# A view of its own for each indirect store of result rows, in an attention, expert and feed-forward kernel on one core

## The chip, the core and the metric

The kernel runs on one core of a Trainium2 chip. The metric is the device time of one execution in microseconds (us), lower is better. A profiled execution gives the span of the core (first to last instruction) and the rows quoted below. Engines are named as in the profile: PE is the matrix engine (TensorE), PEld its weight loads, DVE the vector engine, ACT the scalar engine, POOL the GpSimd engine, SP the engine that issues most transfers. A "q" behind a name (POOLq) is that engine's sequencer.

## The reference

Three parts follow one another. First an attention between 512 tokens and 32 state rows per batch and head, in both directions, gives 4 * (512 + 32) = 2176 rows of 512 numbers. Then a layer of 8 experts with top-1 routing and a capacity, and last a dense feed-forward with a gated activation. Cut to what matters here:

```python
logits = x @ w_gate
expert_idx = np.argmax(logits, axis=1)
# each expert takes at most `capacity` rows, in order; the others keep a zero row
h = np.maximum(np.einsum('ecd,edf->ecf', disp, w1), 0.0)
y = np.einsum('ecf,efd->ecd', h, w2)
out[i] = gate_w[i] * y[expert_idx[i], pos[i]]      # kept rows, the rest are zero
# then, row by row
h = x @ w_in
g = h * np.clip(h + 3.0, 0.0, 6.0) / 6.0
return g @ w_out                                   # 2176 x 512, float32
```

## The kernel before, in words

`phase1` does the attention and the routing, in an order written out by hand (`ORDER`). It leaves the rows in DRAM (`x_rows`) and, for each expert, lists of row numbers. `full` then works through the lists in pieces of 256 rows: an indirect load gathers the rows (L858), two layers of matmuls do the expert (L903, L921), and the result is written, turned, into `y_pad` with the row number of each column beside it. Two half-filled pieces are done apart (L1268, L1294).

From about 231 us on the dense feed-forward runs over `y_pad`. Its rows are no longer in token order; they are packed in `NCS = 7` chunks of 256 columns. Chunks 0 and 1 are done together, 2, 3 and 4 one after the other, and the last 448 columns (`NJ`) as one joint chunk of four parts, the last of which has 64 rows. For each of 16 slices `m` of the hidden layer, `sums3` (L1328) gives the hidden values, `act3` (L1340 to L1348) the activation, split in a high and a low part, and `mm4` (L1366) or `mm4_j` (L1375) adds into the accumulators `po`, four PSUM banks.

When the sixteenth slice of a chunk is added, `put` (L1508 to L1521) takes one accumulator of 128 rows: it scales it into a tile `o` in SBUF, on ACT for the first half of a chunk (L1519) and on DVE for the second (L1517); for the part with 64 rows ACT copies one half and DVE adds the other to it (L1514, L1515). Then POOL issues an indirect store of the rows of `o` to the rows of the output that `fid` names (L1520):

```python
G.indirect_dma_start(out=out, out_offset=bass.IndirectOffsetOnAxis(ap=fid[0:n, t:t + 1], axis=0), in_=o[0:n], in_offset=None,
                     bounds_check=B * (S + NS) - 1, oob_is_err=False)
```

There are 14 such stores: four for chunks 0 and 1, two for each of chunks 2, 3 and 4, and four for the joint chunk. `o` has four buffers, so every fifth tile reuses the first. No kept row is stored twice, and row numbers beyond the output are skipped. Before the first store, three transfers from SP (L1538) fill the whole output with zeros, for the rows that no expert kept.

The waits are put in by the framework, from the tensors that each instruction names. It takes an indirect store as a write of the whole tensor that it is given, here `out`. So each store waits for the one before it to land, beside its wait for its own tile `o`. The order of instructions on every engine is that of the code in this part (`manual_schedule`).

In the last chunk the four stores come as follows (L1575 to L1583): parts 0 and 1 get their last slice and are stored, then part 3 (64 rows, its store needs ACT and then DVE), then part 2. In what follows stores are counted: the eleventh to the fourteenth are those four. Behind the fourteenth POOL reads a flag (L1633), branches over a loop that this input does not need (L1634), and takes part in the closing wait of all engines (L1675).

Of the kernel before, what the change touches and what calls it, by code (L numbers as in the profile page):

```python
# [6 lines left out]

F32 = mybir.dt.float32
F32R = mybir.dt.float32r
# [573 lines left out]
NCS = 7  # L583
# [16 lines left out]
def full(ctx, tc, x, state, w_gate, w1, w2, capacity, w_in, w_out, out, dbg=None):  # L600
    nc = tc.nc
    V, A, G, T = nc.vector, nc.scalar, nc.gpsimd, nc.tensor
# [331 lines left out]
    def y_out(y, idt, row, n=2):  # L934
        V.tensor_copy(y[:, 0:n, DM:YR], idt[:, 0:n].unsqueeze(2).broadcast_to([128, n, YR - DM]))
        if n == 2:
            nc.sync.dma_start(out=y_pad[row, :].rearrange("(t p) c -> p t c", t=2), in_=y)
        else:
            nc.sync.dma_start(out=y_pad[row, :], in_=y[:, 0])
# [498 lines left out]
    for s in range(N0, NF):  # L1438
        last = s + 1 == NF
        p, n = PAIRS.get(s), PAIRS.get(s + 1)  # L1440
# [64 lines left out]

    mw = ctx.enter_context(tc.tile_pool(name="mw", bufs=1, reuse_waits="tile"))

    def put(po, fid, t, half=False):  # L1508
        o = mw.tile([128, DM], F32, name="o", bufs=4)
        n = 64 if half else 128  # L1510
        if half:

            s = mw.tile([128, DM], F32, name="o", bufs=4)
            A.activation(out=s[0:64], in_=po[64:128], func=AF.Copy, scale=C6)  # L1514
            V.scalar_tensor_tensor(out=o[0:64], in0=po[0:64], scalar=C6, in1=s[0:64], op0=ALU.mult, op1=ALU.add)  # L1515
        elif t:
            V.tensor_scalar(out=o, in0=po, scalar1=C6, scalar2=None, op0=ALU.mult)  # L1517
        else:
            A.activation(out=o, in_=po, func=AF.Copy, scale=C6)  # L1519
        G.indirect_dma_start(out=out, out_offset=bass.IndirectOffsetOnAxis(ap=fid[0:n, t:t + 1], axis=0), in_=o[0:n], in_offset=None,  # L1520
                             bounds_check=B * (S + NS) - 1, oob_is_err=False)  # L1521

    def finish(late):
        lm, ls, lg, lpo = late
        for c in ls:
            mm4(lm, *lg[c], lpo[c])
            if lm == 15:
                put(lpo[c][0], ft[c][0][2], 0)
                put(lpo[c][1], ft[c][0][2], 1)
# [46 lines left out]
    for t in range(2):  # L1576
        mm4_j(15, gj[15], pj, (t,))
        put(pj[t], jid[0], t)
# [22 lines left out]
    def l_rows(i, r, e, t):  # L1601
# [28 lines left out]
        V.tensor_copy(yT[:, 0, 0:DM], ps)  # L1630
        y_out(yT, idt, bass.ds(i * 256 + (YL + 128 * t), 128), 1)

    jn = nc.values_load(trips[0:1, 2:3], min_val=0, max_val=NE + NL)  # L1633
    with tc.If(jn > 0):  # L1634
        j0 = nc.values_load(trips[0:1, 1:2], min_val=0, max_val=NE)
# [44 lines left out]
```

## Time and profile before

| what | value |
|---|---|
| runs of the kernel | 551.84, 876.65, 552.94 us; median 552.94 us |
| the profiled execution's own time | 549.64 us |
| its span | 547.9 us |
| granted clock of TensorE, mean | 0.993 of full speed |
| PE busy | 524.8 us, 96% of the span |
| POOL busy | 143.0 us, 26% of the span |
| DMA from POOL's queue | 2208 packets, 7.38 MB |

The span runs from the first to the last instruction; 549.64 - 547.9 = 1.74 us of the execution lie outside it. Busy times count work, not waiting. A row such as "[2.73 <-DMA out_dram<-o,fid]" says that the engine sat idle for 2.73 us before the instruction and what ended that idle time. The duration of an indirect store on POOL is the time in which POOL prepares the transfer; the time to its landing is told apart, from the issue until the data are in place.

### The profile page before, as it was taken

What the parts mean: (1) busy time and instruction counts of PE and PEld (TensorE: products, weight loads), DVE (VectorE), ACT (ScalarE), POOL (GpSimd) and SP (SyncE); (2) the same over time, 40 slices, a digit from 0 to 9 for tenths busy, and PEclk for the clock granted to TensorE, in tenths of its full rate; (3) what the DMA queues carried; (4) which work ended last, traced back from release to release, by engine and by line L of the source; (5) the groups of instructions that cost most, each with busy time, mean ns of one, the idle gap of its engine ahead of it and who ended that gap; (6) DMA issues with size and microseconds to landing.
All of it is one profiled execution on the core that took longest, in us unless ns stands there. A gap on an engine that the chain in (4) does not pass through costs nothing.

```text
span 547.9 us, 10114 instructions
## 1 busy us (share of the span) xinstructions
PE 524.8 (96%) x3772; PEld 461.7 (84%) x3772; DVE 300.1 (55%) x721; ACT 219.0 (40%) x465; POOL 143.0 (26%) x202
## 2 busy tenths in 40 slices
PE   5999999999999999999999999999999999999990
PEld 3666899969699899999998889999999998888880
DVE  5889884369437854667878842243343343332340
ACT  4888742146024413244444443343333343332240
POOL 2657464016101100157767611000001001000002
PEclk9999999999999999999999999999999999999997
DMA  6755628979898954349644211011011010000001
GB/s 135 178 191 185 244 96 254 383 264 338 281 384 299 335 214 140 113 131 360 189 146 143 71 58 39 2 40 38 1 39 39 1 31 29 10 1 1 0 16 56
DMA packets 52170, 75.00 MB, mean 137 GB/s; under 512 B 23089, under 2 KB 31537, under 8 KB 51602
## 3 DMA queue, kind: packets, MB, share of 16 engines
q1 hardware_dynamic: 49362, 66.30, 36.4%
q0 software_dynamic: 2208, 7.38, 4.1%
q8 instruction: 32, 0.52, 0.4%
q10 hardware_dynamic: 544, 0.59, 0.3%
q14 instruction: 24, 0.20, 0.1%
HBM read 70.62 MB, written 16.23 MB: 159 GB/s over the span
## 4 chain that ended last, share of the span: by engine, by line
PE 44%; issue 36%; DMA 8%; DVE 6%; ACT 2%; SPq 2%; POOL 2%; POOLq 0%; DVEq 0%; ACTq 0%
PE pm L903 11%; PE pm L921 10%; DMA out_dram<-o,fid 5%; PE p L1328 5%; PE po L1366 4%; PE pss L903 2%; PE pm L1294 2%; PE pm L1268 2%; PE pss L921 2%; DVE v L1150 1%; DVE g L1341 1%; SPq L100 1%; PE psX L400 1%; DMA st<-in_moe_w_in_dram 1%; DMA xb<-x_rows,ecol 1%
## 5 line engine op out<-in xcount | busy, mean ns | idle before, releaser
L1328 PE MATMUL p<-yT,wh 128*128 128x256 f32 (+1 forms) x768 | 116.7, 294 | 0.0
L1328 PEld LDWEIGHTS p<-yT,wh 128*128 128x128 f32 x768 | 109.2, 188 | 7.8
L1341 DVE SCALAR_TENSOR_TENSOR g<-u,p 128x256 f32<-128x256 f32 x110 | 44.9, 408 | 110.7 <-ACT u L1340 110.6
L1340 ACT ACTIVATE u<-p,b 128x256 f32<-128x256 f32 x110 | 51.1, 464 | 103.5 <-PE p L1328 103.5
L1342 ACT CAST gh<-g 128x256 fp32r<-128x256 f32 x110 | 43.9, 399 | 79.6 <-DVE g L1341 79.6
L1520 POOL DMA_INDIRECT out_dram<-o,fid x14 | 13.6, 973 | 216.0 <-ACT o L1519 191.0
L1328 PE MATMUL p<-yT,wl 128*128 128x256 f32 (+1 forms) x384 | 66.7, 296 | 0.9 <-POOL wl L1165 0.9
L1366 PE MATMUL po<-wh,gh 128*128 128x512 f32 x156 | 61.2, 392 | 0.0
L1366 PE MATMUL po<-wh,gl 128*128 128x512 f32 x156 | 61.2, 392 | 0.0
L1366 PE MATMUL po<-wl,gh 128*128 128x512 f32 x156 | 61.0, 391 | 0.0
L903 PE MATMUL pm<-xt,w1h 128*128 128x256 f32 x320 | 57.9, 282 | 0.9 <-DVE id L872 0.9
L1328 PEld LDWEIGHTS p<-yT,wl 128*128 128x128 f32 x384 | 55.3, 189 | 2.5 <-POOL wl L1165 1.5
L903 PEld LDWEIGHTS pm<-xt,w1h 128*128 128x128 f32 x320 | 48.8, 188 | 4.0 <-issue 2.9
L1348 DVE TENSOR_TENSOR gl<-g,gh 128x256 fp32r<-128x256 f32 x84 | 34.5, 411 | 32.2 <-ACT gh L1342 32.2
L921 PE MATMUL pm<-hth,w2h 128*128 128x256 f32 x160 | 45.0, 281 | 0.0
L921 PE MATMUL pm<-htl,w2h 128*128 128x256 f32 x160 | 44.6, 279 | 0.0
L921 PE MATMUL pm<-hth,w2l 128*128 128x256 f32 x160 | 44.6, 279 | 0.0
L903 PE MATMUL pm<-xt,w1l 128*128 128x256 f32 x160 | 44.0, 279 | 0.0
L1165 POOL TENSOR_TENSOR wl<-v,wh 128x1024 fp32r<-128x1024 f32 x14 | 34.4, 2455 | 35.6 <-ACT wh L1164 35.2
L1366 PEld LDWEIGHTS po<-wh,gl 128*128 128x128 f32 x156 | 29.3, 188 | 7.1 <-POOL gl L1348 0.6
L1348 POOL TENSOR_TENSOR gl<-g,gh 128x256 fp32r<-128x256 f32 x26 | 25.4, 975 | 30.2 <-ACT gh L1342 30.2
L1366 PEld LDWEIGHTS po<-wh,gh 128*128 128x128 f32 x156 | 29.4, 188 | 3.8
(316 smaller groups left out, 947.2 us busy)
## 6 DMA issues: line engine op xcount, KB each, us to landing
raw<-in_moe_w_dram SPq DMA_DIRECT2D x80, 512.0 KB
st<-in_moe_w_in_dram SPq DMA_DIRECT2D x16, 512.0 KB
st<-in_moe_w_out_dram SPq DMA_DIRECT2D x16, 512.0 KB
x_rows<-xrow SPq DMA_DIRECT2D x4, 1072.0 KB
xb<-in_x_dram SPq DMA_DIRECT2D x32, 128.0 KB
yg<-y_pad SPq DMA_DIRECT2D x13, 258.0 KB
out_dram<-zt SPq DMA_DIRECT2D x2, 1536.0 KB
y_pad<-y SPq DMA_DIRECT2D x5, 516.0 KB
```

Of the source, the lines that this page charges most:

```text
L903: T.matmul(ps[:, j], W1[l][k][:, ls], xT[r][:, k], start=n == 0, stop=n == 11)
L921: T.matmul(ps[:, j], W2[l][k // 2][:, k % 2, ls], hT[k // 2][r][:, k % 2], start=k == 0 and i == 0, stop=k == 7 and i == 2)
L1165: (V if m in (0, 2) else G).tensor_tensor(out=wl, in0=v, in1=wh.bitcast(F32), op=ALU.subtract)
L1268: T.matmul(ps[0 if p else n][s:s + w, :], th[:, 128 * k + s:128 * k + s + w], raws[k, g][:, 512 * n:512 * n + 512], start=i == 0, stop=i == 3)
L1294: T.matmul(ps[s:s + m, :], th[:, a:a + m], raws[k // 2, g][:, 512 * (k % 2) + 256 * n:512 * (k % 2) + 256 * n + w], start=k == 0, stop=k == 7)
L1328: T.matmul(out, w[:, 128 * k:128 * k + 128], r(k), start=n == 0, stop=n == 11)
L1340: A.activation(out=u, in_=ps, func=AF.Relu, bias=b3)
L1341: V.scalar_tensor_tensor(out=g, in0=u, scalar=6.0, in1=ps, op0=ALU.min, op1=ALU.mult)
L1342: A.copy(gh[:, 0:w], g)
L1348: eng.tensor_tensor(out=gl, in0=g[:, 0:n], in1=gh[:, 0:n].bitcast(F32), op=ALU.subtract)
L1366: T.matmul(po[t], l[:, ls], r[:, 512:1024], start=m == 0 and i == 0, stop=m == 15 and i == 2)
L1520: G.indirect_dma_start(out=out, out_offset=bass.IndirectOffsetOnAxis(ap=fid[0:n, t:t + 1], axis=0), in_=o[0:n], in_offset=None, bounds_che ...
```

## The change

The output is divided into 2 * NCS = 14 views by a call that declares them to be without overlap. Each call of `put` takes one of them for its store; all 14 are used up by the 14 stores. Each view still names the whole output as far as addresses go, so the rows go where they went before. In the loop behind L1633 the list is empty and `out` itself is used.

```diff
+from concourse.bass_types import dram_disjoint_views
...
+    outs = dram_disjoint_views(out, 2 * NCS)
+
     def put(po, fid, t, half=False):
...
-        G.indirect_dma_start(out=out, out_offset=bass.IndirectOffsetOnAxis(ap=fid[0:n, t:t + 1], axis=0), in_=o[0:n], in_offset=None,
+        G.indirect_dma_start(out=outs.pop() if outs else out, out_offset=bass.IndirectOffsetOnAxis(ap=fid[0:n, t:t + 1], axis=0), in_=o[0:n], in_offset=None,
                              bounds_check=B * (S + NS) - 1, oob_is_err=False)
...
+    outs.clear()
     jn = nc.values_load(trips[0:1, 2:3], min_val=0, max_val=NE + NL)
```

No instruction is added, removed or moved on any engine. What differs are the waits of POOL's stores. In the rows below DMASW and a digit is one of the eight semaphores that POOL's transfers raise in turn when they land, Activation and DVE are the engines that wrote the tile `o`, and the DMAHW semaphores of the first row are those of the zero fill. POOL's instructions of the last four stores before:

```order
271 L1520 DMA out_0_dram<-o_6790,fid_5921 2176x512 [waits DMASW7_49,Activation_49]
272 L1520 DMA out_0_dram<-o_6798,fid_5921 2176x512 [waits DMASW0_49,DVE_49]
273 L1520 DMA out_0_dram<-o_6809,fid_5922 2176x512 [waits DMASW1_49,DVE_49]
274 L1520 DMA out_0_dram<-o_6825,fid_5922 2176x512 [waits DMASW2_49,Activation_49]
275 L1633 TENSOR_LOAD trips_70
```

and now:

```order
271 L1523 DMA out_0_dram<-o_6790,fid_5921 2176x512 [waits DMASW0_49,Activation_49]
272 L1523 DMA out_0_dram<-o_6798,fid_5921 2176x512 [waits DMASW1_49,DVE_49]
273 L1523 DMA out_0_dram<-o_6809,fid_5922 2176x512 [waits DMASW2_49,DVE_49]
274 L1523 DMA out_0_dram<-o_6825,fid_5922 2176x512 [waits DMASW3_49,Activation_49]
275 L1637 TENSOR_LOAD trips_70
```

Before, each waits for the semaphore of the store just ahead of it (the first of the 14 raises number 6, the next number 7, then 0 and so on). Now each waits for the semaphore that it will itself raise, whose last use was eight stores earlier. The stores of chunks 0 and 1 and of chunk 2 on POOL before:

```order
261 L1520 DMA out_0_dram<-o_4763,fid_3467 2176x512 [waits DMAHW5_49,DMAHW6_49,DMAHW1_49,Activation_49]
262 L1520 DMA out_0_dram<-o_4768,fid_3467 2176x512 [waits DMASW6_49,DVE_49]
263 L1520 DMA out_0_dram<-o_4779,fid_3524 2176x512 [waits DMASW7_49,Activation_49]
264 L1520 DMA out_0_dram<-o_4784,fid_3524 2176x512 [waits DMASW0_49,DVE_49]
265 L1520 DMA out_0_dram<-o_5235,fid_4429 2176x512 [waits DMASW1_49,Activation_49]
```

and now:

```order
261 L1523 DMA out_0_dram<-o_4763,fid_3467 2176x512 [waits DMAHW5_49,DMAHW6_49,DMAHW1_49,Activation_49]
262 L1523 DMA out_0_dram<-o_4768,fid_3467 2176x512 [waits DVE_49]
263 L1523 DMA out_0_dram<-o_4779,fid_3524 2176x512 [waits Activation_49]
264 L1523 DMA out_0_dram<-o_4784,fid_3524 2176x512 [waits DVE_49]
265 L1523 DMA out_0_dram<-o_5235,fid_4429 2176x512 [waits Activation_49]
```

The first store keeps its waits for the zero fill; those behind it on the same engine now wait for their tile alone. On ACT the last scaling copy, which fills the `o` of the fourteenth store, has the same waits before and now, one of them for the landing of the eleventh store, whose buffer it reuses:

```order
511 L1519 ACTIVATE o_6790<-po_6178 128x512 [waits DMASW4_49,PE_49]
512 L1514 ACTIVATE o_6810<-po_6181 64x512 [waits DMASW6_49,PE_49]
513 L1519 ACTIVATE o_6825<-po_6180 128x512 [waits DMASW0_49,PE_49,Activation_49]
514 L1633 TENSOR_LOAD trips_70 [waits DVE_49]
515 L1634 COMPARE_AND_BRANCH
```

Nothing moved there; the eleventh store raises number 0.

## Rows read from the trace of the kernel before

**Rows 1.** The page: the store's group (busy, mean ns, idle before, releaser).

```profile
L1520 POOL DMA_INDIRECT out_dram<-o,fid x14 | 13.6, 973 | 216.0 <-ACT o L1519 191.0
```

**Rows 2.** Busy time by stretch; columns: length, engines' busy us, clock, DMA share, GB/s.

```profile
320.00:341.00 21.00, 21.00 (x133) 18.93 (x132) 7.29 (x16) 7.27 (x16) 3.96 (x4) 1.00 0.13 51
341.00:530.00 189.00, 189.00 (x1084) 169.07 (x1083) 66.16 (x179) 66.08 (x156) 5.83 (x6) 1.00 0.06 17
535.00:539.00 4.00, 0.42 (x2) 0.00 (x0) 0.00 (x0) 0.60 (x1) 0.97 (x1) 1.00 0.20 72
540.00:548.00 8.00, 0.00 (x0) 0.00 (x0) 0.00 (x0) 0.00 (x0) 1.30 (x2) 0.52 0.16 50
```

**Rows 3.** POOL in order of time from 470 us: start, duration, instruction, idle before.

```profile
532.19 0.97 POOL L1520 DMA_INDIRECT out_dram<-o,fid  x1 [67.37 <-ACT o L1519]
535.89 0.97 POOL L1520 DMA_INDIRECT out_dram<-o,fid  x1 [2.73 <-DMA out_dram<-o,fid]
539.40 0.92 POOL L1520 DMA_INDIRECT out_dram<-o,fid  x1 [2.54 <-DMA out_dram<-o,fid]
542.78 0.97 POOL L1520 DMA_INDIRECT out_dram<-o,fid  x1 [2.46 <-DMA out_dram<-o,fid]
```

**Rows 4.** The chain that ended last, its final stretch: start, duration, what.

```profile
532.19 2.93 DMA out_dram<-o,fid
...
535.89 2.74 DMA out_dram<-o,fid
...
539.40 2.61 DMA out_dram<-o,fid
542.01 0.02 issue
```

**Rows 5.** Who waited for whom from 520 us on: total us, times, longest.

```profile
POOL out_dram L1520 <- DMA out_dram<-o,fid: 7.7, 3, 2.7
```

**Rows 6.** Line L1520 over the whole span: who waited for it, and landing times.

```profile
  POOL out_dram L1520: 19.9, 7
...
DMA to landing us min/median/max: 2.6/2.7/4.6
```

**Rows 7.** ACT in order of time, 531 to 537 us, same columns as rows 3.

```profile
531.31 0.60 ACT L1519 ACTIVATE o<-po 128x512 f32<-128x512 f32 x1 [0.69 <-PE po L1375]
...
535.50 0.60 ACT L1519 ACTIVATE o<-po 128x512 f32<-128x512 f32 x1 [1.53 <-PEq L1634]
```

**Rows 8.** DVE in order of time, 531 to 537 us.

```profile
532.00 0.69 DVE L1517 TENSOR_SCALAR o<-po 128x512 f32<-128x512 f32 x1 [0.92 <-PE po L1375]
534.01 0.68 DVE L1515 SCALAR_TENSOR_TENSOR o<-po,o 64x512 f32<-64x512 f32 x1 [1.31 <-ACT o L1514]
```

**Rows 9.** PE in order of time, its last matmul.

```profile
535.03 0.39 PE L1375 MATMUL po<-wh,gl 128*128 128x512 f32 x1
```

**Rows 10.** POOL around 90 us: two gathers behind each other.

```profile
89.91 1.01 POOL L858 DMA_INDIRECT xg<-x_rows,col  x1 [0.61 <-POOL col L1187]
91.22 1.00 POOL L858 DMA_INDIRECT xg<-x_rows,col  x1 [0.30 <-issue]
```

**Rows 11.** Line L858, all its gathers: landing times.

```profile
DMA to landing us min/median/max: 3.6/6.2/7.1
```

**Rows 12.** Line L1634, sequencers: duration ns min/median/max, first and last start.

```profile
L1634 POOLq EVENT_SEMAPHORE  x4: 17/17/43, 543.1 to 543.4; - x4
...
L1634 PEldq EVENT_SEMAPHORE  x2: 51/51/51, 535.5 to 535.6; - x2
L1634 ACTq EVENT_SEMAPHORE  x2: 17/17/17, 536.1 to 536.2; - x2
...
L1634 POOLq INC_SWDGE_SEM  x1: 757/757/757, 543.5 to 543.5; - x1
```

**Rows 13.** Line L1675, the closing wait of all engines, same columns.

```profile
L1675 SPq EVENT_SEMAPHORE  x14: 17/28/1372, 544.2 to 547.8; - x14
...
L1675 POOLq DRAIN  x3: 46/107/2511, 544.6 to 547.6; - x3
```

## The prediction

> **What bounds the kernel now.** I read the busy time by stretch first. TensorE is busy for 21.00 of 21.00 us between 320 and 341 us and for 189.00 of 189.00 us between 341 and 530 us [rows 2]. Stores that wait in those stretches cannot cost time through TensorE, since it never stops. Its last matmul ends at 535.03 + 0.39 = 535.42 us [rows 9], and the span ends at 547.9 us, so 12.5 us of the kernel have no matmul in them. The reader should look at this stretch and nowhere else.
>
> POOL's order of time says what fills it [rows 3]: the last four stores begin at 532.19, 535.89, 539.40 and 542.78 us. The last three each sat idle for about 2.5 us until a transfer of an earlier store had landed; in the list of waits from 520 us on that is 7.7 us in three times [rows 5]. The chain that ended last runs through the same transfers, 2.93, 2.74 and 2.61 us [rows 4]. Over the whole span seven stores waited so, 19.9 us in all, and no other instruction is listed as waiting for a store [rows 6]. So 19.9 - 7.7 = 12.2 us of these waits lie under a busy TensorE and are worth nothing, and the 7.7 us at the end are in the open.
>
> The page would mislead here: it puts most of the store's idle time, 191.0 of 216.0 us, to ACT [rows 1]. That is POOL having nothing to do until the next chunk is ready.
>
> **What the change is worth, step by step.** The order on every engine is unchanged; what goes are the waits of a store for the landing of the one ahead. The wait that stands there now is for a store eight back. For the eleventh to the fourteenth those are the third to the sixth, landed long before. So a store now begins when its tile is written and POOL is free. The working, with two small steps from rows:
>
> - From a written tile to the store's start: the eleventh store had no landing to wait for. Its copy on ACT ended at 531.31 + 0.60 = 531.91 us [rows 7] and it began at 532.19 us [rows 3]: 0.28 us.
> - From the end of one indirect transfer on POOL to the start of the next with nothing to wait for: two gathers show 0.30 us, from 89.91 + 1.01 = 90.92 to 91.22 us [rows 10].
>
> Eleventh store: 532.19 us as before, POOL free at 533.16. Twelfth: its copy on DVE ends at 532.00 + 0.69 = 532.69 us [rows 8], which with 0.28 is 532.97, but POOL is free only at 533.16, so 533.16 + 0.30 = 533.46 us, done at 534.43. Thirteenth: DVE ends at 534.01 + 0.68 = 534.69 us [rows 8], so 534.97 us, done at 535.94 with 0.97. Fourteenth: ACT ends at 535.50 + 0.60 = 536.10 us [rows 7], so 536.38 us; POOL would allow 535.94 + 0.30 = 536.24. The fourteenth store is held by its own data again, and begins 542.78 - 536.38 = 6.40 us earlier. That is less than the 7.7 us of waits because its tile is written late.
>
> Behind it nothing changes: from its start to the end of the span are 547.9 - 542.78 = 5.12 us, in which POOL leaves the branch (543.1 to 543.4), raises its transfers' semaphore and drains, while SP waits for the landing [rows 12, 13]. The other engines reach that point by 535.6 (PE) and 536.2 us (ACT) [rows 12], ahead of the fourteenth store even now, so POOL's end moves forward whole. The span becomes 541.50 us, and the execution 549.64 - 6.40 = 543.24 us.
>
> **Covers and bounds.** The last copy on ACT reuses the tile of the eleventh store, whose landing at 532.19 + 2.93 = 535.12 us [rows 4] now hides behind TensorE's end at 535.42. If that landing took 4.6 us, the longest of any store [rows 6], it would come at 536.79; with the present 535.50 - 535.12 = 0.38 us behind it the copy would start at 537.17, 1.67 us late, and 4.73 us would be left of the gain. I cost this at nothing: the twelfth store would start only 1.27 us after the eleventh, and a store takes little of the DMA engines, 0.20 of 4 us or 0.8 us [rows 2].
>
> For the fourteenth store's start the lower end is its tile, 536.10 us, a gain of 6.68. The upper end is the step that a store needs after a landing, from 542.01 [rows 4] to 542.78 us, 0.77 instead of 0.28: a gain of 5.91. I take 0.28, since the semaphore of eight stores ago has long been raised. Its landing with another store in flight is shown by no row. The nearest are the stores with 2.6 to 4.6 us [rows 6]; the gathers, which run under heavier traffic, took up to 7.1 us [rows 11]. Against the usual 2.7 that is nothing to 1.9 us later, or 4.4 us at the far end. I take 2.7, because stores that begin 1.41 to 1.51 us apart have room for 0.8 us of transfer each. The first ten stores I cost at nothing on either side: they bunch up at 322 to 331 us, but TensorE waits for none of them. In the stretch from 341 to 530 us POOL's six pieces of work are the stores themselves [rows 2].
>
> On what the removed wait consists of, the rows show 2.93, 2.74 and 2.61 us from issue to landing, of which POOL's own part is 0.97, and the third, with 64 rows, is hardly shorter [rows 3, 4]. The Trainium skill, "DMA: Bandwidth & Descriptors", section "Anatomy of one DMA — SWDGE (gpsimd) path", gives a fixed 2.0 us for a transfer plus its bytes at 436 GB/s, and says that most of the fixed part is the confirmation of the write. By that 128 rows of 2 KB would take 2.6 us and 64 rows 2.3 us; three such steps with 0.77 us behind each put the fourteenth store of the kernel before at 542.0 us, and the gain would be 5.6 us by the page against 6.40 by the rows. The rows decide.
>
> **Rivals.** (a) The transfers are served one behind another, whatever POOL does: the eleventh lands at 535.12, and each later one adds its part behind POOL's, 2.74 - 0.97 = 1.77, then 2.61 - 0.92 = 1.69, then again about 1.75 us, so the fourteenth lands at 540.3 us instead of 542.78 + 2.7 = 545.5. The gain is 5.2 us, 544.4 us. For it speaks that no row shows two stores in flight; against it, that the data take only 0.8 us of each landing. The Trainium skill, the same page, section "SWDGE vs HWDGE vs iDMA", says that only one such queue is allocated; no row here shows what two stores in it do.
>
> (b) The cover on ACT is lost, as worked out above: 4.73 us, 544.9 us. Against it stands the margin, 0.30 us to TensorE's end, and that only a store under other traffic took 4.6 us.
>
> (c) The waits go but the end stays, because the closing stretch was set by something else: 549.6 us. Against it: PE and ACT are through by 536.2 us, and SP's and POOL's closing rows lie behind the last store [rows 12, 13]. That the change does not do what it says comes to the same time; the waits in the order speak against it.
>
> (d) Slower: the drain on POOL's sequencer at the end. It takes 2.511 us [rows 13] where every store but the last has been waited for by the next. If it has to settle each store that POOL never waited for on its own, the last chunk has three more of them: 3 * 2.51 = 7.53 us against 6.40 gained, 550.8 us, 1.1 us slower. It decides from the third further store on (two cost 5.02). For it speaks only that the drain is long; against it, that when it starts, 544.6 - 6.40 = 538.2 us, the thirteenth store, begun at 534.97, would have landed.
>
> **How the numbers follow.** The forecast has 0.78, (a) 0.10, (b) 0.05, (c) 0.04, (d) 0.03. The profiled execution stands 3.30 us under the median of the runs shown, 552.94 us; the runs are what is compared, so I take the gain off the median: 552.94 - 6.40 = 546.5 us. The low end is the profiled execution's level with the largest gain, 549.64 - 6.68 = 543.0 us. The high end covers (a) at 547.7 and (b) at 548.2 us with 0.8 to 1.3 us to spare for a landing somewhat longer than either: 549.0 us. A measurement of this kernel can tell about 2% from no change, 11.1 us. Every case, (d) included, lies within that, so 0.95 for no change; 0.02 for faster, which would need nearly twice the wait that is there; 0.03 for slower, because (d) has no upper bound in a row and one of the three runs, 876.65 us, shows that a run can lie far off.
>
> **What would show it.** In the profile after, the last four stores should begin near 532.2, 533.5, 535.0 and 536.4 us, with the fourteenth released by ACT's copy and no store released by a landing. TensorE should end at 535.4 us and the span about 5.1 us behind the fourteenth store's start. The earlier stores of chunks 0 and 1 should come closer together with TensorE still at 21.00 of 21.00 us. Wrong would be: landings one behind another, 1.7 us apart (a); ACT's last copy released by a store (b); the same 12.5 us behind the last matmul (c); a drain above 2.5 us (d).

## The result, and the profile after

The changed kernel took 543.31 us (median of 4 runs, 542.94 to 544.66), the kernel before 552.39 us in the same comparison (median of 4, one of them the run of 876.65 us). The ratio leaves out that run, which lies far above the others, and is not the quotient of the two medians: it is 0.9867, with a 95% interval from 0.9842 to 0.9892. That is faster by about 1.3%, clear of noise, but under the 2% that were named as a bound. The forecast was 546.5 us with a range of 543.0 to 549.0; the measured time lies 0.3 us above its lower end, and two of the four runs (542.94 and 542.96 us) lie just below it.

POOL in order of time, from 460 us on, in the changed kernel (start, duration, instruction, idle before and what ended it), answers to [rows 3]:

```profile
533.48 0.97 POOL L1523 DMA_INDIRECT out_dram<-o,fid  x1 [69.57 <-ACT o L1522]
534.76 0.97 POOL L1523 DMA_INDIRECT out_dram<-o,fid  x1 [0.30 <-issue]
536.26 0.92 POOL L1523 DMA_INDIRECT out_dram<-o,fid  x1 [0.53 <-DVEq L1638]
537.67 0.97 POOL L1523 DMA_INDIRECT out_dram<-o,fid  x1 [0.49 <-ACTq L1638]
```

The reader is to see the brackets: no store is released by a landing any more, and 2.5 to 2.7 us of idle time have become 0.3 to 0.5. The twelfth store is held by POOL itself (0.30), the thirteenth by DVE's tile, the fourteenth by ACT's. The names with "q" in two of the brackets are the next steps of the sequencers that wrote those tiles. ACT, DVE and PE around the same stores, answering to [rows 7 to 9]:

```profile
533.30 0.69 DVE L1520 TENSOR_SCALAR o<-po 128x512 f32<-128x512 f32 x1 [0.93 <-PE po L1376]
535.30 0.68 DVE L1518 SCALAR_TENSOR_TENSOR o<-po,o 64x512 f32<-64x512 f32 x1 [1.31 <-ACT o L1517]
...
536.80 0.60 ACT L1522 ACTIVATE o<-po 128x512 f32<-128x512 f32 x1 [1.53 <-PEq L1638]
...
536.33 0.39 PE L1376 MATMUL po<-wh,gl 128*128 128x512 f32 x1
```

The last matmul ends at 536.72, ACT's copy at 537.40, the fourteenth store begins at 537.67. Before, the store began 542.78 - 535.42 = 7.36 us behind the last matmul, now 0.95 us: 6.41 us less. Line L1523 over the whole span, against [rows 6]:

```profile
who waited for it (us, times):
busy tenths in 40 slices 0000000000000000000000001001001000100002
DMA to landing us min/median/max: 2.7/2.7/4.5
```

Nobody is listed any more under those who waited for a store, where seven stores stood with 19.9 us. The landings over the whole span are what they were, 2.7 us in the median. One in the closing stretch is longer: the thirteenth store's took 3.2 us, where it took 2.6 before; more on it below. The stretches before, by busy time, against [rows 2]:

```profile
320.00:341.00 21.00, 21.00 (x133) 18.96 (x132) 6.88 (x16) 6.86 (x15) 3.94 (x4) 1.00 0.14 51
341.00:530.00 189.00, 189.00 (x1087) 169.26 (x1086) 65.90 (x179) 65.75 (x155) 5.83 (x6) 1.00 0.05 17
```

TensorE was full there before and is full now, while the first four stores have moved together:

```profile
324.08 1.02 POOL L1523 DMA_INDIRECT out_dram<-o,fid  x1 [8.62 <-ACT o L1522]
325.41 0.98 POOL L1523 DMA_INDIRECT out_dram<-o,fid  x1 [0.31 <-DVE o L1520]
326.69 0.97 POOL L1523 DMA_INDIRECT out_dram<-o,fid  x1 [0.30 <-ACT u L1341]
327.96 0.97 POOL L1523 DMA_INDIRECT out_dram<-o,fid  x1 [0.30 <-issue]
```

Before, the same four were these:

```profile
322.78 1.02 POOL L1520 DMA_INDIRECT out_dram<-o,fid  x1 [8.62 <-ACT o L1519]
326.35 0.98 POOL L1520 DMA_INDIRECT out_dram<-o,fid  x1 [2.54 <-DVE g L1341]
331.76 0.98 POOL L1520 DMA_INDIRECT out_dram<-o,fid  x1 [4.44 <-DMA out_dram<-o,fid]
335.29 0.97 POOL L1520 DMA_INDIRECT out_dram<-o,fid  x1 [2.55 <-DVE gl L1348]
```

From the first to the fourth it was 12.5 us; now it is 3.9 us. Two of the old brackets name DVE, though with a line (L1341, L1348) that does not write the tile of the store. Without the wait for the store ahead those two idle times are 0.3 us, so they were waits for a landing as well: nine stores waited so, with 25.0 us, and not the seven with 19.9 that the list names. That the first four gave nothing shows in one number, which the experiments give again: from the start of the first store to the end of the last matmul it is 535.42 - 322.78 = 212.64 us before and 536.72 - 324.08 = 212.64 us now.

### The profile page after: what moved, and what is told of

Its sections match the earlier page's. It is cut to its first block, busy times and chain, and to the rows that moved or that the text cites. A ratio compares the mean times of both kernels' runs of the same rounds, so it can differ in the third digit from the quotient of the medians.

```text
span 542.9 us, 10107 instructions
## 1 busy us (share of the span) xinstructions
PE 526.1 (97%) x3772; PEld 462.6 (85%) x3772; DVE 301.0 (55%) x721; ACT 219.2 (40%) x465; POOL 143.7 (26%) x202
## 4 chain that ended last, share of the span: by engine, by line
PE 53%; issue 25%; DMA 10%; DVE 7%; POOL 2%; ACT 2%; SPq 0%; POOLq 0%; DVEq 0%; ACTq 0%
PE p L1329 11%; PE po L1367 10%; PE pm L922 8%; PE pm L904 8%; DMA raw<-in_moe_w_dram 3%; PE pss L904 2%; DMA st<-in_moe_w_out_dram 2%; PE pm L1295 2%; PE psx L277 2%; PE pss L922 2%; PE pss L285 2%; DVE v L1151 2%; DMA y_pad<-xb 2%; DVE g L1342 1%; DVE v L1147 1%
## 5 line engine op out<-in xcount | busy, mean ns | idle before, releaser
L1341 ACT ACTIVATE u<-p,b 128x256 f32<-128x256 f32 x110 | 51.1, 465 | 103.5 <-PE p L1329 103.5
L1523 POOL DMA_INDIRECT out_dram<-o,fid x14 | 13.6, 972 | 209.6 <-ACT o L1522 206.4
```

Source lines behind the costliest of these rows:

```text
L1341: A.activation(out=u, in_=ps, func=AF.Relu, bias=b3)
L1523: G.indirect_dma_start(out=outs.pop() if outs else out, out_offset=bass.IndirectOffsetOnAxis(ap=fid[0:n, t:t + 1], axis=0), in_=o[0:n], in ...
```

## The experiments

All times in the table are from the profiled execution of each kernel, in us. "PE end" is the end of the last matmul; the span moves with the stretches ahead of the first store, which differ from run to run by about 3 us, so the closing stretch is compared from PE end.

| kernel | first store | PE end | last store | span | PE end to last store | last store to end | PE end to end |
|---|---|---|---|---|---|---|---|
| before | 322.78 | 535.42 | 542.78 | 547.9 | 7.36 | 5.1 | 12.5 |
| after | 324.08 | 536.72 | 537.67 | 542.9 | 0.95 | 5.2 | 6.2 |
| e1_same | 324.91 | 537.55 | 538.58 | 543.8 | 1.03 | 5.2 | 6.3 |
| e2_last4 | 323.43 | 536.06 | 537.02 | 542.1 | 0.96 | 5.1 | 6.0 |
| e3_first10 | 324.73 | 537.37 | 544.94 | 550.0 | 7.57 | 5.1 | 12.6 |
| e4_last2 | 323.38 | 536.02 | 541.50 | 547.0 | 5.48 | 5.5 | 11.0 |
| e5_last3 | 325.87 | 538.51 | 541.63 | 546.7 | 3.12 | 5.1 | 8.2 |
| e6_three_tiles | 324.13 | 536.78 | 539.11 | 544.3 | 2.33 | 5.2 | 7.5 |
| e7_without_14th | 323.53 | 536.17 | 535.71 | 541.7 | -0.46 | 6.0 | 5.5 |

In all nine kernels the first store's start and PE end lie 212.63 to 212.65 us apart.

**Where the gain comes from: the last four stores, or the first ten too.** The theory was that the whole gain lies in the closing stretch. The rival was that the first ten stores add to it, since the first comparison gave 552.39 - 543.31 = 9.1 us where 6.4 were worked out. The edit, with the condition that e2_last4 has; e3_first10 has `nput[0] <= 10` instead, and e1_same is the changed kernel as it is:

```diff
     outs = dram_disjoint_views(out, 2 * NCS)
+    nput = [0]
...
+        nput[0] += 1
+        dst = outs.pop() if outs and nput[0] > 10 else out
...
-        G.indirect_dma_start(out=outs.pop() if outs else out, out_offset=bass.IndirectOffsetOnAxis(ap=fid[0:n, t:t + 1], axis=0), in_=o[0:n], in_offset=None,
+        G.indirect_dma_start(out=dst, out_offset=bass.IndirectOffsetOnAxis(ap=fid[0:n, t:t + 1], axis=0), in_=o[0:n], in_offset=None,
```

> The changed kernel once more, in more rounds, for a narrower ratio. Theory (the whole gain is the closing stretch): 6.3 to 6.4 us of about 551, a ratio of 0.988 to 0.989. Rival (the first ten stores, which also lost their waits, give some too): 7 us or more, 0.987 or less. In the profile the last matmul's end to the end of the span should be 6.2 us again, whatever the stretches before it do.

> Views only for the eleventh to fourteenth store; the first ten wait for one another as before. Theory: all of the gain stays, last matmul to end of span 6.2 us, ratio equal to that of the changed kernel, 0.988 to 0.989. Rival (first ten stores matter): the ratio is 0.001 to 0.002 higher than that of the changed kernel in the same call.

> Views only for the first ten stores; the last four wait for one another as before. Theory: nothing gained, last matmul to end of span 12.5 us, ratio 1.000 within 0.002. Rival: the first ten give about 1 us, ratio 0.998, with a shorter stretch between 320 and 530 us.

Measured, against the same 17 runs of the kernel before (median 550.23 us): e1_same 544.59 us, ratio 0.9876 (0.9844 to 0.9907); e2_last4 543.76 us, 0.9863 (0.9832 to 0.9894); e3_first10 550.48 us, 0.9998 (0.9979 to 1.0017). POOL around the first and the last stores in e2_last4:

```profile
323.43 1.02 POOL L1526 DMA_INDIRECT out_dram<-o,fid  x1 [8.63 <-ACT o L1525]
...
336.35 0.97 POOL L1526 DMA_INDIRECT out_dram<-o,fid  x1 [2.55 <-DVE gl L1349]
...
534.11 0.97 POOL L1526 DMA_INDIRECT out_dram<-o,fid  x1 [0.30 <-issue]
535.61 0.92 POOL L1526 DMA_INDIRECT out_dram<-o,fid  x1 [0.53 <-DVEq L1641]
537.02 0.97 POOL L1526 DMA_INDIRECT out_dram<-o,fid  x1 [0.49 <-ACTq L1641]
```

The first four stores are spread over 12.9 us, about as in the kernel before, the last stores follow each other as in the changed one, and the time is that of the changed kernel. In e3_first10 it is the other way round, again in POOL's order of time:

```profile
534.14 0.97 POOL L1526 DMA_INDIRECT out_dram<-o,fid  x1 [69.58 <-ACT o L1525]
538.05 0.97 POOL L1526 DMA_INDIRECT out_dram<-o,fid  x1 [2.94 <-DMA out_dram<-o,fid]
541.56 0.92 POOL L1526 DMA_INDIRECT out_dram<-o,fid  x1 [2.54 <-DMA out_dram<-o,fid]
544.94 0.97 POOL L1526 DMA_INDIRECT out_dram<-o,fid  x1 [2.45 <-DMA out_dram<-o,fid]
```

The rival falls, by the profiles more than by the times. The times cannot part the two: the intervals are 0.002 to 0.003 to either side, as wide as the difference that the rival forecast, and e1_same's 0.9876 lies between the theory's 0.988 and the rival's 0.987. (These ratios, too, are not the quotients of the medians; by the medians e1_same gains 5.6 us and e2_last4 6.5.) But from the first store to PE end all kernels need the same 212.6 us whether their first ten stores wait or not, and behind PE end e2_last4 needs 6.0 us, e1_same 6.3 and e3_first10 12.6. So ten of the thirteen removed waits are worth nothing. All three intervals of kernels with the gain hold the ratio that a gain of 6.4 us gives, 1 - 6.4 / 550.23 = 0.988. Of the 2.7 us by which the first 9.1 exceed 6.4, 2.2 are the level of the runs of before, 552.39 in a median that takes in the 876.65, against 550.23 us in 17 further runs.

**What one removed wait is worth.** The same edit with `nput[0] > 12` (e4_last2: one landing wait gone) and `nput[0] > 11` (e5_last3: two gone).

> Views only for the last two stores, so one landing wait is gone, that of the fourteenth store. Theory (each removed wait trades landing plus a step for POOL's own 0.92 plus 0.30 us): the fourteenth starts 1.22 us after the thirteenth instead of 3.38, gain 2.2 us, last matmul to end 10.3 us. Rival (the transfers are served one behind another): the start moves, but the landing of the fourteenth comes about 1.7 us behind the thirteenth's, and the gain is about 1.7 us with a landing time of 3 us or more.

> Views for the last three stores, two landing waits gone. Theory: the stores follow each other at 1.27 and 1.22 us once the eleventh has landed, POOL being the bound and no longer a landing; the fourteenth starts 4.4 us earlier against the last matmul than in the kernel before, last matmul to end 8.1 us. With all three waits gone it is 6.3 and no longer 6.6, since the tile of the fourteenth is the limit there. Rival (served one behind another): landings 1.7 us apart, 8.9 us.

One execution each, POOL in order of time, first e4_last2, then e5_last3:

```profile
540.27 0.92 POOL L1526 DMA_INDIRECT out_dram<-o,fid  x1 [2.54 <-DMA out_dram<-o,fid]
541.50 0.98 POOL L1526 DMA_INDIRECT out_dram<-o,fid  x1 [0.30 <-POOLq L1641]
```

```profile
539.13 0.97 POOL L1526 DMA_INDIRECT out_dram<-o,fid  x1 [2.88 <-DMA out_dram<-o,fid]
540.41 0.92 POOL L1526 DMA_INDIRECT out_dram<-o,fid  x1 [0.30 <-issue]
541.63 0.98 POOL L1526 DMA_INDIRECT out_dram<-o,fid  x1 [0.31 <-DMA out_dram<-o,fid]
```

Without the wait a store follows the one ahead by 1.22 to 1.28 us, POOL's own 0.92 to 0.97 and a gap of 0.30, instead of 3.4 to 3.7. (The last bracket names a landing, but the gap is 0.31 us, that of POOL alone; e5_last3's fourteenth store waits for no landing.) The starts came as the theory said. In e5_last3 so did the end, 8.2 us behind PE end against 8.1 expected. In e4_last2 it was 11.0 against 10.3. Of the 0.7 us, 0.27 lie in the twelfth store, which started 3.97 us behind the eleventh where the kernel before has 3.70, and 0.4 behind the fourteenth store, whose landing took 3.5 us instead of 2.7. The rival, transfers one behind another, had named a landing of 3 us or more, so e4_last2 alone would speak for it. But it would need the same in e5_last3, where three stores follow each other as closely. The DMA queues (packets, MB, share) while the fourteenth store's data moved, in e4_last2 and then in e5_last3:

```profile
q0 software_dynamic: 80, 0.26, 31.5%
q14 instruction: 1, 0.01, 0.9%
```

```profile
q0 software_dynamic: 80, 0.26, 42.6%
```

In both there are the 80 packets of one store. In e4_last2 there is a packet of instructions beside them, in e5_last3 none, and there the thirteenth and fourteenth store land after 2.6 and 2.7 us, at about 543.0 and 544.3. So two stores in flight 1.22 us apart do not lengthen each other's landing, and the rival falls. The first three stores of the changed kernel say the same: 1.33 and 1.28 us apart, they land after 2.8, 2.7 and 2.7 us. That the packet of instructions is what cost e4_last2 its 0.8 us is argued from the two lying together; no run took it away. For it speaks that the trace records a landing in sixteen parts, and that fifteen of them came by 544.24 us and only one late, at 544.97. Against it, a packet of the same queue moved while the fourteenth store of the kernel before was in flight, and that store landed after the usual 2.7 us.

**The tiles' cover.** The edit: `o` and the helper tile `s` with `bufs=3` instead of 4.

```diff
-        o = mw.tile([128, DM], F32, name="o", bufs=4)
+        o = mw.tile([128, DM], F32, name="o", bufs=3)
...
-            s = mw.tile([128, DM], F32, name="o", bufs=4)
+            s = mw.tile([128, DM], F32, name="o", bufs=3)
```

> The changed kernel with three instead of four buffers for the scaled tiles: DVE's write of the thirteenth tile now has to wait for the landing of the eleventh store, and ACT's last copy for DVE. Theory (the landings are covered only while four tiles are there): DVE starts near 0.4 us after that landing, about 1.4 us later than in the changed kernel, and the fourteenth store and the end come 1.3 us later, 7.5 us from the last matmul. Rival (landings play no part any more): 6.2 us as in the changed kernel.

One execution; DVE, ACT and POOL in order of time:

```profile
536.92 0.68 DVE L1518 SCALAR_TENSOR_TENSOR o<-po,o 64x512 f32<-64x512 f32 x1 [2.87 <-DMA out_dram<-o,fid]
...
537.70 0.60 ACT L1522 ACTIVATE o<-po 128x512 f32<-128x512 f32 x1 [2.36 <-DVEq L1638]
...
539.11 0.98 POOL L1523 DMA_INDIRECT out_dram<-o,fid  x1 [0.30 <-POOLq L1638]
```

Now a landing is in the chain again: DVE waits 2.87 us for the eleventh store, ACT waits for DVE, and the end comes 7.5 us behind PE end, as expected. The size came right in part by luck, since two terms were off against each other: DVE was expected 0.4 us behind the landing and began 0.1 us behind it, but the landing took 3.3 us where the changed kernel has 2.9. The landing wait did not vanish with the views; it is covered by the four tiles. Three would give back 1.3 us of the 6.3.

Four tiles cover it with nothing to spare. In e1_same, with four, the eleventh store began at 534.32 us; its landing and ACT's last copy:

```profile
DMA to landing us min/median/max: 3.3/3.3/3.3
...
537.71 0.60 ACT L1522 ACTIVATE o<-po 128x512 f32<-128x512 f32 x1 [1.60 <-PEq L1638]
```

It landed at about 537.6 us, just behind the last matmul's end at 537.55, and the copy started 0.16 us behind that end instead of 0.08. The fourteenth store began 0.08 us later for it, 1.03 us behind PE end against 0.95.

**What the end follows.** The changed kernel with the fourteenth store left out:

```diff
+        nput[0] += 1
+        if nput[0] == 14:
+            return
         G.indirect_dma_start(out=outs.pop() if outs else out, out_offset=bass.IndirectOffsetOnAxis(ap=fid[0:n, t:t + 1], axis=0), in_=o[0:n], in_offset=None,
```

> The changed kernel without the fourteenth store, so 128 rows of the output are left at zero. Theory (the end follows the last store by a fixed 5.2 us): the thirteenth store starts 0.46 us before the last matmul's end, so the span ends 4.8 us behind the last matmul, 1.4 us less than in the changed kernel. Rival (POOL's drain settles something else): the drain ends as far behind the last matmul as it does with the store, 6.2 us to the end.

The span ended 5.5 us behind PE end, between the theory's 4.8 and the rival's 6.2. The last store, now the thirteenth, was followed by 6.0 us instead of 5.2. The closing wait's rows of e7_without_14th, then of the changed kernel (sequencer instructions, duration ns min/median/max, first and last start):

```profile
L1683 SPq EVENT_SEMAPHORE  x14: 17/28/2315, 537.1 to 541.7; - x14
L1683 POOLq EVENT_SEMAPHORE  x4: 17/17/17, 540.6 to 541.6; - x4
L1683 POOLq DRAIN  x3: 46/107/3440, 537.1 to 541.2; - x3
```

```profile
L1679 SPq EVENT_SEMAPHORE  x14: 17/28/1383, 539.0 to 542.8; - x14
L1679 POOLq EVENT_SEMAPHORE  x4: 17/17/17, 541.6 to 542.8; - x4
L1679 POOLq DRAIN  x3: 46/254/2467, 539.1 to 542.6; - x3
```

POOL's drain is not a fixed time. It started 2.0 us earlier in e7_without_14th, at 537.1, and lasted longer, 3.44 us against 2.47, until 540.6. SP's long wait, which is the wait for the last landing, ends near 537.1 + 2.3 = 539.4 there and near 539.0 + 1.4 = 540.4 in the changed kernel; in both the drain ends 1.2 us later. So the end follows the last landing, not the last store's start. The thirteenth store landed about 3.7 us after its start in e7_without_14th; in the changed kernel its landing took 3.2. Two packets of instructions moved in that stretch of e7_without_14th as well, which the queues show from 536.8 to 539.4 us:

```profile
q0 software_dynamic: 48, 0.13, 23.0%
q8 instruction: 1, 0.02, 3.1%
q14 instruction: 1, 0.01, 1.3%
```

Neither theory held as it stood: in place of the theory's fixed 5.2 us behind the last store's start, the span ends 2.0 to 2.5 us behind the last landing in all nine profiles, 542.9 - 540.4 = 2.5 in the changed kernel, 541.7 - 539.4 = 2.3 in e7_without_14th, 2.0 in e4_last2.

## Why the prediction was right, point by point

- **What bounds the kernel.** It was the stretch without matmuls. From the first store to PE end nothing changed, 212.64 us, though the first ten stores lost their waits; e3_first10, with those alone, gave 0.9998. That the waits of the first ten stores were worth nothing is shown. Their sum was read too low: with the two waits that the list puts to DVE it is 17.3 of 25.0 us, not 12.2 of 19.9.
- **The four starts.** Worked out as 533.46, 534.97 and 536.38 us for the last three, with the eleventh at 532.19. Against the eleventh that is 1.27, 2.78 and 4.19 us; measured 1.28, 2.78 and 4.19 us. The two small steps, 0.28 us from tile to store and 0.30 us from store to store, carried over. That the fourteenth is held by its tile and not by POOL is in its bracket.
- **The sum.** 6.40 us were expected between PE end and the fourteenth store, 6.41 came. The tail behind it was taken as 5.12 us and came as 5.2; PE end to the end of the span lost 6.3 us. The span itself was to be 541.50 us and is 542.9, because everything from the first store on came 1.3 us later in this execution: that store began at 324.08 instead of 322.78 us.
- **The cover on ACT** held in the changed kernel: its last copy started 536.80 - 536.72 = 0.08 us behind the last matmul, as before. Rival (b) was a real mechanism, as e6_three_tiles shows, and four tiles are only just enough. The eleventh store's landing was costed at 2.93 us and took 2.9 to 3.3 in the nine profiles, which uses up the margin of 0.30 us: e1_same lost 0.08 us by it, the small end of what (b) described. Against (b) the prediction held that only a store under other traffic took 4.6 us. While that store was in flight the queues show its own 80 packets and one packet of instructions; what made it long stays open.
- **Rival (a)**, transfers one behind another, is refuted by e5_last3, and by the changed kernel itself: its thirteenth store landed at about 536.26 + 3.2 = 539.5 us and its fourteenth at 537.67 + 2.7 = 540.4, 0.9 us apart where (a) has 1.7. Rival (c), an end set by something else, is refuted by the result.
- **Rival (d)**, a drain that settles each store, rested on reading 2.511 us as work. The drain waits for the last landing. That no store waits for the one ahead any more cost it nothing: 2.467 us after, 2.511 before.
- **The step that was off** is the level. The gain was taken off 552.94 us, the median of the three runs shown. Seventeen further runs of the kernel before have a median of 550.23 us, 2.7 us lower; 550.23 - 6.40 = 543.8 us, and the changed kernel measured 543.31, and 544.59 in the second comparison. The size of the gain was right and the level was 2.7 us too high; seen from the result, the profiled execution's own 549.64 us, which gives 543.24, would have been the better base. That 543.31 lies inside the range is owed to that second level, from which the low end of 543.0 was taken; from the median's level the largest gain ends at 552.94 - 6.68 = 546.3 us. The bound of 2% for what a measurement can tell was too wide: the interval is a quarter of a percent to either side.
- **The price by the Trainium skill**, "DMA: Bandwidth & Descriptors", section "Anatomy of one DMA — SWDGE (gpsimd) path", an estimate of 2.6 us for 128 rows and 2.3 for 64, would have made the gain 5.6 us. The traces do not agree with it: the last stores of the kernel before landed after 2.7 to 2.9 us with 128 rows and 2.6 with 64. The rows' landings gave 6.40, and 6.41 was measured.

## What to carry to other kernels

A framework that orders scattered stores by the tensor they name makes each wait for the landing of the last, and where no engine works any more behind them these waits add up at the end; look at the stretch behind the last matmul and at who ended POOL's idle time there, not at the sum of all such waits. A removed wait is worth the time to landing less what the next limit leaves: here the 3.4 to 3.7 us from one store to the next shrank to POOL's 1.2 to 1.3 where POOL was the limit, and for the last store to the time at which its tile was written. Before trusting the gain, count the buffers behind the stores: they are what hides the landings once the stores no longer wait for each other. Here four were just enough for landings of up to 3.3 us.

## What the runs showed of the hardware that was not expected

- Stores in flight together do not, by that alone, slow each other here. In e5_last3 three that start 1.28 and 1.22 us apart land after 2.7, 2.6 and 2.7 us, as stores alone do (2.7 us with 128 rows, 2.6 with 64).
- The closing drain on POOL's sequencer is a wait, not work: between 2.4 and 3.9 us long in the nine profiles, its length depends on when it begins. It ended 1.2 us behind the last landing in eight of them and 1.6 us behind it in the kernel before; why it is more there is open.
- Some landings are longer, and a packet of instructions moved beside nearly all of these: 2.9 to 3.3 us for the eleventh store of all nine profiles, 3.2 to 3.7 for the thirteenth of the four profiles in which it followed 1.5 us behind the twelfth, 4.3 to 5.0 for one store near 330 us in eight of the nine. In the long ones of the closing stretch one or two of the sixteen parts of a landing were late and the others in time. But such a packet stood also beside landings of 2.7 us, as with the fifth store of the changed kernel and the fourth of e6_three_tiles. That it is the cause is not shown; no run took it away.
